# Scores' operand of a spectral and expert-retrieval kernel: float32 products in place of split bfloat16 products

## The chip, the cores and the metric

The kernel runs on one core of a Trainium2 chip. The metric is the device time of one execution in microseconds (us); the time before is 1265.43 us, the median of three runs (1265.05 to 1265.48). Five engines work side by side, each on a queue of its own that it goes through in order: TensorE (PE in the profile; its weight loads are shown apart as PEld), VectorE (DVE), ScalarE (ACT), GpSimd (POOL) and SyncE (SP), which here issues the DMAs. They wait for each other through semaphores.

## The reference, cut to what matters

Four sublayers, two kinds in turn, on 2048 tokens of 512 values: a Fourier mixing by DFT matrices, and a retrieval of experts by keys.

```python
q = jnp.einsum("nd,dhc->nhc", xf, w_q)      # w_q: (512, 32 heads, 2 * 128)
q1 = q[..., :dk]
q2 = q[..., dk:]
s1 = jnp.einsum("nhd,ed->nhe", q1, k1)      # k1, k2: (16, 128)
s2 = jnp.einsum("nhd,ed->nhe", q2, k2)
...
x = x + _A_ref(_layernorm(x, axis=-1), ...)   # y = Real(DFT_seq(DFT_hidden(x)))
x = x + _B_ref(_layernorm(x, axis=-1), ...)
x = x + _A_ref(_layernorm(x, axis=-1), ...)
x = x + _B_ref(_layernorm(x, axis=-1), ...)
```

The scores s1 and s2 of a token are its 512 values times w_q times the keys. The kernel never makes q. It first multiplies w_q by the keys, which gives one operand of 512 x (2 halves x 32 heads x 16 keys), and then multiplies the tokens by that operand. The two best of 16 scores are picked for each half and head, so the operand is kept to nearly float32 accuracy.

## The kernel before, in words

**Tiling.** Tokens lie in 16 tiles of 128. All products that need accuracy are made with operands held as a high and a low part (float32r, names ending in h and l): high x high, low x high, high x low. The DFT over the sequence goes by units of 256 tokens (`seq_unit`, from line 434): per unit 16 pieces of `cseq` are loaded by SP (`raw`, L454), split by ScalarE (`ch`, L458) and VectorE (`cl`, L462), and multiplied with the layer-normed tokens `xh`, `xl` on TensorE (L518, three products of 512 columns per step). The DFT over the hidden dimension (L615), the scores (L694, L698), the expert products and what follows are made token tile by token tile (`token_tile`).

**Set-up.** Before the first scores can be made, `setup` prepares the constants: the hidden DFT's matrices, the operand of the scores (`wh`, `wl`) and the experts' matrices. The operand is made from w_q in 32 groups of two heads of one half (16 groups for each of the two key matrices). A group is 512 KB in a tile `wr` (128 x 2 x 512 float32), loaded by SP (L315). For each group VectorE takes the upper 16 bits of each float32 as a bfloat16 part and subtracts it (L381, tile `w1`), then does that once more on what is left (L384). The keys have been split into three bfloat16 parts once (`kb`, 48 columns, L356 and L358). TensorE then visits the group: for each of 4 blocks of the model dimension and 2 heads it multiplies the three parts of w_q (as the weights, 128 x 128) with the 48 columns of the keys' parts, 24 products in all (L392). VectorE adds up the three key parts out of PSUM (L397, tile `ws`), ScalarE casts that to the high part (`wh`, L404) and VectorE subtracts to get the low part (`wl`, L407).

**What sets the order.** Every piece of work is an `Op` with an engine, an estimated duration, what it comes after, which buffers it takes and gives back, and a priority. `Plan.run` simulates the engines with these estimates and gives the order in which the instructions are issued; nothing is reordered afterwards. The durations are therefore no part of the arithmetic, but change the order. A visit of a group has the highest priority on TensorE once its inputs are planned to be there; sequence products fill the time between. Since each engine is in order, a visit whose inputs come later than planned holds up all the products that stand behind it. Buffers are counted in `BUFS`: five `wr` tiles, two sets of `wp` (`w1` and `ws`), four PSUM tiles `bank`, which the visits share with the token tiles, and four `acc` for the sequence DFT. The scores of the first token tile wait for all of the set-up (`setup_done`).

Other lines that are named below: L664 transposes a token tile's values (128 x 128 float32 through an identity), L725 multiplies them by the experts' operand (256 columns), L943 multiplies half-precision one-hot matrices in two column halves of the array, and L978, for the last token tile only, picks values with plain float32 products of 64 weight columns and 16 moving columns, in the same two halves.

Of the kernel before, what the change touches and what calls it, by code (L numbers as in the profile page):

```python
# [20 lines left out]
KD = D // P  # L21
# [3 lines left out]
SP = 1  # L25
NPC = NT // SP
NSC = 1
H = 32
E = 16
# [40 lines left out]
class Plan:  # L70
# [10 lines left out]
    def op(self, engine, us, fn, after=(), take=(), last=(), prio=(0, 0), lag=0.0, behind=()):  # L81
        o = Op(len(self.ops), engine, us, fn, [a for a in after if a is not None], list(take), list(last), prio, lag,
               list(behind))
        for h in o.last:
            h.users += 1
        self.ops.append(o)
        return o
# [59 lines left out]

MM512, MM256, TR32, TR16, MMG = 0.2275, 0.1203, 0.12, 0.057, 0.0156  # L150


def dve(n, rate=1):
    return 0.069 + n / (0.96e3 * rate)


def act(n):
    return 0.09 + n / 1.2e3


def load(kb):
    return kb / 256 * 1.05
# [3 lines left out]
def spectral_peer_kernel(ctx: ExitStack, tc, x_in, cseq, ctile, dhid, wq, k1t, k2t, ut, vm, out):  # L166
    nc = tc.nc
# [5 lines left out]
    ctx.enter_context(tc.manual_schedule())  # L173


    BUFS = {"acc": 4, "bank": 4, "raw": 4, "c": 3, "p": 1, "row": 4, "wr": 5, "wp": 2,
            "tok": 3, "sc": 1, "eq": 1, "act": 3, "q": 2, "top": 1, "qt": 1, "lr": 4, "gt": 1, "pp": 1, "gdr": 2, "bn": 1}
    plan = Plan(BUFS)

# [5 lines left out]
    wh = const.tile([P, KD, 2, H, E], F32R, name="wh")  # L185
    wl = const.tile([P, KD, 2, H, E], F32R, name="wl")
# [53 lines left out]
    def ln_stats(get, i, after, prio):  # L240
        bn, h = {}, Hold("bn")

        def f0():
            bn[0] = apool.tile([P, 6], F32, name="bn", bufs=BUFS["bn"])
            nc.vector.bn_stats(bn[0], get())
# [44 lines left out]
    xload = {}  # L290
    for i in range(NT):
        def first(i=i):
            h, t = Hold("wr"), {}

            def f():
                t[0] = setup_pool().tile([P, D], F32, name="wr", bufs=BUFS["wr"])
                nc.sync.dma_start(t[0], x_in[i * P:(i + 1) * P, :])
# [8 lines left out]
    setup_done = []  # L306

    def setup():
        def wr(src, prio, after):
            h, t = Hold("wr"), {}  # L310

            def f():
                t[0] = setup_pool().tile([P, 1024], F32, name="wr", bufs=BUFS["wr"]).rearrange(
                    "p (a b) -> p a b", b=src.shape[2])
                nc.sync.dma_start(t[0], src)  # L315

            return op("SP", load(512), f, [after], take=[h], prio=prio, lag=2.3), h, lambda: t[0]

        def parts(hi, lo, src, sign, prio):
            a, h, r = wr(src, prio, xload[8])  # L320

            def f0():
                if sign > 0:
                    nc.scalar.copy(hi, r())
                else:
                    nc.scalar.mul(hi, r(), -1.0)

            def f1():
                if sign > 0:
# [13 lines left out]


        kb, kready = [], []
        for hf, kt in enumerate((k1t, k2t)):
            kr = {}

            def f0(hf=hf, kt=kt, kr=kr):
                kr[0] = setup_pool().tile([P, 3, E], F32, name=f"kr{hf}")  # L350
                nc.sync.dma_start(kr[0][:, 0, :], kt)

            def f1(hf=hf, kr=kr):
                t = setup_pool().tile([P, 3, E], BF16, name=f"kb{hf}")
                for n in range(3):
                    nc.vector.tensor_copy(t[:, n, :], kr[0][:, n, :])  # L356
                    if n < 2:
                        nc.vector.tensor_sub(kr[0][:, n + 1, :], kr[0][:, n, :], t[:, n, :])  # L358
                kb.append(t)

            a = op("SP", 0.2, f0, prio=(1, hf), lag=2.3)
            kready.append(op("DVE", 0.9, f1, [a], prio=(1, hf)))


        HG = 2

        def halves(t, u):
            return t.bitcast(BF16).rearrange("p a (d u) -> p a d u", u=2)[:, :, :, u]

        def upper(t):  # L370
            return halves(t, 1)

        for hf in range(2):
            for g in range(H // HG):
                prio = (3, hf, g)
                a0, hw, r0 = wr(wq[hf, g * HG:(g + 1) * HG].rearrange("h c d -> c h d"), prio, xload[NT - 1])
                hp, hb, t = Hold("wp"), Hold("bank"), {}

                def f1(r0=r0, t=t):
                    t[1] = setup_pool().tile([P, HG, D], F32, name="w1", bufs=BUFS["wp"])  # L380
                    nc.vector.tensor_sub(t[1], r0(), upper(r0()))  # L381

                def f2(t=t):
                    nc.vector.tensor_sub(halves(t[1], 0), t[1], upper(t[1]))  # L384

                def f3(hf=hf, r0=r0, t=t):
                    t[3] = bank([P, KD * HG, 64])
                    ws = (upper(r0()), upper(t[1]), halves(t[1], 0))
                    for k in range(KD):
                        for a in range(HG):  # L390
                            for n, w in enumerate(ws):
                                nc.tensor.matmul(t[3][:, k * HG + a, :3 * E], w[:, a, k * P:(k + 1) * P],  # L392
                                                 kb[hf], start=(n == 0), stop=(n == 2), skip_group_check=True)

                def f4(t=t):
                    t[4] = setup_pool().tile([P, KD, HG, E], F32, name="ws", bufs=BUFS["wp"])
                    nc.vector.tensor_reduce(t[4].rearrange("p k a e -> p (k a) e"),  # L397
                                            t[3][:, :, :3 * E].rearrange("p b (n e) -> p b e n", e=E),
                                            axis=AX.X, op=ALU.add)

                hs = slice(g * HG, (g + 1) * HG)

                def f5(hf=hf, hs=hs, t=t):
                    nc.scalar.copy(wh[:, :, hf, hs, :], t[4])  # L404

                def f6(hf=hf, hs=hs, t=t):
                    nc.vector.tensor_sub(wl[:, :, hf, hs, :], t[4], as32(wh[:, :, hf, hs, :]))  # L407

                a1 = op("DVE", dve(1024), f1, [a0], take=[hp], prio=prio)
                a2 = op("DVE", dve(1024), f2, [a1], prio=prio)  # L410
                a3 = op("PE", 24 * 0.0255 + 0.1, f3, [a2, kready[hf]], take=[hb], last=[hw], prio=(0, 0))
                a4 = op("DVE", dve(384), f4, [a3], last=[hb], prio=prio)
                a5 = op("ACT", act(128), f5, [a4], prio=prio)
                setup_done.append(op("DVE", dve(128), f6, [a5], last=[hp], prio=prio))
        setup_done.append(parts(uh, ul, ut.rearrange("(k p) e -> p k e", p=P), 1, (4, 0)))
        setup_done.append(parts(vh, vl, vm.rearrange("(k p) e -> p k e", p=P), 1, (4, 1)))
        setup_done.extend(xready[0, i] for i in range(NT))
        return dft

    dft_done = setup()  # L420


# [138 lines left out]
    last = {}  # L561
# [629 lines left out]
```

## Time and profile before

| | |
|---|---|
| time, median of 3 runs | 1265.43 us (1265.05 to 1265.48) |
| time of the profiled execution | 1266.79 us |
| its span, first to last instruction | 1264.9 us |
| TensorE busy, longest group | L518, three groups of 1072 products, 398 to 408 us each |
| TensorE's granted clock | 1.00 throughout |
| visits of the changed code (L392) | 768 products, 58.8 to 181.8 us |
| loads of w_q (L315) | 32 of 512 KB, 4.1 us to landing |
| HBM read over the span | 107.36 MB |

A line of the grouped view names the kernel's line, the engine, the operation, the tiles (out<-in), the partitions and elements, and the count; then the busy time in us and the mean duration of one in ns; then the idle time of the engine just before, and what ended it. In the timeline the columns are start and duration in us, engine, line, operation, tiles and count, with the idle time before in brackets. The stretches give the busy time of each engine in us with its number of instructions, then TensorE's granted clock, the share of the DMA engines and GB/s. Products on TensorE overlap: one that shows 0.39 us is followed by the next after 0.23, so it is the step from start to start that counts, not the duration. PE busy is therefore near to full wherever products follow each other at any pace.

### The profile page before, as it was taken

The numbers are of one execution on the slowest core, as the hardware profiler recorded it, in microseconds if no ns is written. First come the engines' busy times: TensorE is split into PE (matmuls) and PEld (weight loads), VectorE is DVE, ScalarE is ACT, GpSimd is POOL, SyncE is SP. The second block draws the span as 40 slices with busy tenths as digits, with TensorE's granted clock in tenths as the row PEclk, the third lists the DMA queues.
The fourth block names the chain that finished last, engine by engine and source line by source line (L and its number), as shares of the span: only waits on it lengthen the run. The fifth ranks groups of instructions, "written<-read, shape, count | busy, mean of one in ns | idle before, by whom it ended". The sixth has DMA issues, their size and how long they took to land.

```text
span 1264.9 us, 20684 instructions
## 1 busy us (share of the span) xinstructions
PE 1250.8 (99%) x7804; PEld 1036.8 (82%) x7804; DVE 994.2 (79%) x2257; ACT 466.5 (37%) x966; POOL 45.7 (4%) x71
## 2 busy tenths in 40 slices
PE   9999999999999999999999999999999999999998
PEld 6777778887888888899878887888888888888886
DVE  8899998988887957779884378695685847778598
ACT  7522243343433333333563333333332433333232
POOL 2010000000000000000000000000000000000000
PEclk9999999999999999999999999999999999999999
DMA  7866541333233241413455204314142331414201
GB/s 235 268 197 213 180 150 34 92 70 65 67 84 76 76 101 50 112 39 88 121 133 135 67 26 104 81 59 109 42 108 51 93 91 51 108 43 110 58 9 35
DMA packets 224101, 121.18 MB, mean 96 GB/s; under 512 B 136448, under 2 KB 202496, under 8 KB 224000
## 3 DMA queue, kind: packets, MB, share of 16 engines
q1 hardware_dynamic: 224000, 119.85, 35.4%
q8 instruction: 61, 1.00, 0.3%
q14 instruction: 40, 0.33, 0.1%
HBM read 107.36 MB, written 12.45 MB: 95 GB/s over the span
## 4 chain that ended last, share of the span: by engine, by line
PE 71%; DVE 16%; issue 6%; DMA 2%; ACT 2%; SPq 1%; POOL 1%; POOLq 0%; DVEq 0%; ACTq 0%
PE acc L518 39%; PE bank L615 11%; PE bank L694 7%; PE bank L698 4%; PE bank L725 3%; DVE cl L462 2%; DVE w L384 2%; PE bank L1044 2%; DVE w L381 2%; PE bank L518 1%; PE bank L943 1%; DVE eq L778 1%; PE bank L1048 1%; PE bank L664 1%; POOL stats L260 1%
## 5 line engine op out<-in xcount | busy, mean ns | idle before, releaser
L518 PE MATMUL acc<-ch,xh 128*128 128x512 f32 (+1 forms) x1072 | 407.9, 381 | 0.0
L518 PE MATMUL acc<-ch,xl 128*128 128x512 f32 (+1 forms) x1072 | 397.8, 371 | 0.3 <-DVE xl L287 0.3
L518 PE MATMUL acc<-cl,xh 128*128 128x512 f32 (+1 forms) x1072 | 397.8, 371 | 0.0
L458 ACT CAST ch<-raw 128x512 fp32r<-128x512 f32 x256 | 158.4, 619 | 263.7 <-PE acc L518 227.0
L462 DVE TENSOR_TENSOR cl<-raw,ch 128x512 fp32r<-128x512 f32 x256 | 175.5, 687 | 72.4 <-ACT ch L458 52.9
L518 PEld LDWEIGHTS acc<-cl,xh 128*128 128x128 f32 x1072 | 201.9, 188 | 35.2
L518 PEld LDWEIGHTS acc<-ch,xh 128*128 128x128 f32 x1072 | 202.1, 189 | 32.6 <-issue 1.4
L518 PEld LDWEIGHTS acc<-ch,xl 128*128 128x128 f32 x1072 | 202.5, 189 | 31.6 <-DVE xl L287 1.0
L615 PE MATMUL bank<-dh,pth 128*128 128x512 f32 (+1 forms) x264 | 102.9, 392 | 0.4 <-ACT pth L543 0.4
L694 PE MATMUL bank<-wh,tok 128*128 128x512 f32 x256 | 100.2, 392 | 1.3 <-ACT sc L955 1.0
L615 PE MATMUL bank<-dl,pth 128*128 128x512 f32 (+1 forms) x264 | 100.6, 383 | 0.0
L694 PE MATMUL bank<-wl,tok 128*128 128x512 f32 x256 | 99.7, 390 | 0.0
L615 PE MATMUL bank<-dh,ptl 128*128 128x512 f32 (+1 forms) x264 | 95.9, 384 | 0.0
L784 DVE TENSOR_TENSOR tmp<-sc 128x512 f32<-128x512 f32 (+1 forms) x66 | 44.4, 672 | 61.7 <-ACT sc L703 60.8
L926 DVE TENSOR_TENSOR lr<-iota,qt 128x1024 f16<-128x1024 f16 x124 | 80.6, 684 | 10.6 <-ACT qt L907 10.6
L260 POOL TENSOR_TENSOR stats<-stats,half 128x1 f32<-128x1 f32 x64 | 44.4, 697 | 1183.7 <-DVE stats L257 1182.5
L778 DVE TENSOR_TENSOR eq<-sc,val 128x1024 f16<-128x1024 f32 (+1 forms) x66 | 78.5, 1190 | 1.5
L703 ACT COPY sc<-bank 128x512 f32<-128x512 f32 x64 | 36.8, 589 | 104.1 <-PE bank L698 73.1
L698 PE MATMUL bank<-wh,tok 128*128 128x512 f32 x256 | 68.5, 389 | 0.0
L800 DVE TENSOR_TENSOR eq<-eq 128x256 f16<-128x256 f16 (+3 forms) x198 | 60.0, 303 | 1.6
L615 PEld LDWEIGHTS bank<-dh,pth 128*128 128x128 f32 x264 | 49.6, 188 | 10.4 <-ACT pth L543 0.9
L694 PEld LDWEIGHTS bank<-wh,tok 128*128 128x128 f32 x256 | 48.1, 188 | 11.6 <-ACT raw L271 1.1
(152 smaller groups left out, 1790.7 us busy)
## 6 DMA issues: line engine op xcount, KB each, us to landing
raw<-in_cseq SPq DMA_DIRECT2D x224, 256.0 KB, 2.8
wr<-in_wq SPq DMA_DIRECT2D x32, 512.0 KB, 4.1
raw<-in_ctile SPq DMA_DIRECT2D x32, 256.0 KB, 2.9
wr<-in_x SPq DMA_DIRECT2D x16, 256.0 KB, 3.4
row<-in_x SPq DMA_DIRECT2D x16, 256.0 KB, 3.1
x2d<-row SPq DMA_DIRECT2D x16, 256.0 KB, 2.0
row<-x2d SPq DMA_DIRECT2D x16, 256.0 KB, 3.2
out<-row SPq DMA_DIRECT2D x16, 256.0 KB, 2.3
```

What stands on the lines that cost most here:

```text
L260: nc.gpsimd.tensor_tensor(st[:, 1:2], st[:, 1:2], half, op=ALU.pow)
L458: nc.scalar.copy(t[1], t[0])
L462: nc.vector.tensor_sub(t[2], t[0], as32(t[1]))
L518: nc.tensor.matmul(target(d), w[:, s, d * P:(d + 1) * P], moving(s % per, part), start=(s == 0 and k == 0 and d % blocks == 0), stop=(s == ...
L615: nc.tensor.matmul(t["y", cs.start], w[:, k, c, t0:t0 + P], r[:, c, k, cs], start=(z == 0 and c == 0 and m == 0), stop=(z == len(steps) - ...
L694: nc.tensor.matmul(t["pc", hf], t["th"][:, k, :], r[:, k, hf], start=(k == 0 and r is wh), stop=False)
L698: nc.tensor.matmul(t["pc", hf], t["tl"][:, k, :], wh[:, k, hf], start=False, stop=(k == KD - 1))
L725: nc.tensor.matmul(t["xu"], w[:, k, :], r[:, k, :], start=(m == 0), stop=(m == 3 * KD - 1))
L778: nc.vector.tensor_tensor(t["eq"][:, :, cols], flat("sc")[:, :, cols], val(rank_, cols), op=ALU.is_equal)
L784: nc.vector.tensor_max(t["tmp"][:, :, cols], flat("sc")[:, :8, cols], flat("sc")[:, 8:, cols])
L800: nc.vector.tensor_max(s[:, :m], s[:, :m], s[:, m:2 * m])
L926: nc.vector.tensor_tensor(t["m", hf, r], io2, row_of(r, hf), op=ALU.is_equal)
```

## The change

The operand's groups are multiplied in float32. The keys are kept as they are loaded (`kr`, 128 x 16 float32, for each half). Two groups of w_q (four heads) share one visit of TensorE: 4 heads x 4 blocks = 16 products with 128 columns of float32 weights straight from `wr` and 16 moving columns, into one PSUM tile. ScalarE casts the 256 values per partition to `wh` and VectorE subtracts to get `wl`, both directly from PSUM. The splitting of w_q and of the keys, the reduction and the tiles `w1`, `ws` and `kb` go. `wr` has seven buffers in place of five. There are 16 visits in place of 32, each planned at 16 x 0.105 us (`MM16`), where the old ones were planned at 24 x 0.0255 + 0.1.

```diff
-MM512, MM256, TR32, TR16, MMG = 0.2275, 0.1203, 0.12, 0.057, 0.0156
+MM512, MM256, TR32, TR16, MMG, MM16 = 0.2275, 0.1203, 0.12, 0.057, 0.0156, 0.105
...
-    BUFS = {"acc": 4, "bank": 4, "raw": 4, "c": 3, "p": 1, "row": 4, "wr": 5, "wp": 2,
+    BUFS = {"acc": 4, "bank": 4, "raw": 4, "c": 3, "p": 1, "row": 4, "wr": 7,
...
-            def f1(hf=hf, kr=kr):
-                t = setup_pool().tile([P, 3, E], BF16, name=f"kb{hf}")
-                for n in range(3):
-                    nc.vector.tensor_copy(t[:, n, :], kr[0][:, n, :])
-                    if n < 2:
-                        nc.vector.tensor_sub(kr[0][:, n + 1, :], kr[0][:, n, :], t[:, n, :])
-                kb.append(t)
...
-        HG = 2
+        HG, PG = 2, 2
...
-                def f1(r0=r0, t=t):
-                    t[1] = setup_pool().tile([P, HG, D], F32, name="w1", bufs=BUFS["wp"])
-                    nc.vector.tensor_sub(t[1], r0(), upper(r0()))
-
-                def f2(t=t):
-                    nc.vector.tensor_sub(halves(t[1], 0), t[1], upper(t[1]))
...
-                    for k in range(KD):
-                        for a in range(HG):
-                            for n, w in enumerate(ws):
-                                nc.tensor.matmul(t[3][:, k * HG + a, :3 * E], w[:, a, k * P:(k + 1) * P],
-                                                 kb[hf], start=(n == 0), stop=(n == 2), skip_group_check=True)
-
-                def f4(t=t):
-                    t[4] = setup_pool().tile([P, KD, HG, E], F32, name="ws", bufs=BUFS["wp"])
-                    nc.vector.tensor_reduce(t[4].rearrange("p k a e -> p (k a) e"),
-                                            t[3][:, :, :3 * E].rearrange("p b (n e) -> p b e n", e=E),
-                                            axis=AX.X, op=ALU.add)
...
+                def f0(hf=hf, loads=loads, t=t):
+                    t[0] = bank([P, KD, PG * HG, E])
+                    for m, (_, _, r) in enumerate(loads):
                         for a in range(HG):
+                            for k in range(KD):
+                                nc.tensor.matmul(t[0][:, k, m * HG + a], r()[:, a, k * P:(k + 1) * P], kr[hf],
+                                                 start=True, stop=True)
+
+                def f1(hf=hf, hs=hs, t=t):
+                    nc.scalar.copy(wh[:, :, hf, hs, :], t[0])
+
+                def f2(hf=hf, hs=hs, t=t):
+                    nc.vector.tensor_sub(wl[:, :, hf, hs, :], t[0], as32(wh[:, :, hf, hs, :]))
+
+                n = PG * HG * KD
+                a = op("PE", n * MM16, f0, [m[0] for m in loads] + [kready[hf]], take=[hb], last=[m[1] for m in loads],
+                       prio=(0, 0))
```

Below the change 32 lines are gone, so L518 is L486 there, L615 is L583, L454 is L422, L462 is L430; the new visit is L369, its casts L373 and its subtractions L376.

**TensorE, at the first visit** (about 58 us in the profile of before). Before, the last three products of a token tile's hidden DFT and the first two products of the visit, each with its own weight load; `wr` is the upper part of w_q, `w_683` the two others:

```order
L615 MATMUL bank<-dh,pth 128x512
L615 MATMUL bank<-dl,pth 128x512
L615 MATMUL bank<-dh,ptl 128x512
L392 LDWEIGHTS wr
L392 MATMUL bank<-kb_507,wr 128x48
L392 LDWEIGHTS w_683
L392 MATMUL bank<-kb_507,w_683 128x48
```

and of the change, the whole visit between the same neighbours (a float32 product loads its weights itself, so that no load is listed):

```order
L583 MATMUL bank<-dh,pth 128x512
L583 MATMUL bank<-dl,pth 128x512
L583 MATMUL bank<-dh,ptl 128x512
L369 MATMUL bank<-kr_452,wr 128x16 x16
L583 MATMUL bank<-dh,pth 128x512
```

A visit of 24 products of 48 columns becomes one of 16 products of 16 columns, for twice as many heads.

**VectorE, between two visits** (in the stage from 55 to 182 us of the profile of before). Before, what it does for one group and the next, with one split of a sequence piece (L462) between:

```order
L381 TENSOR_TENSOR w_929<-wr 128x1024
L397 TENSOR_REDUCE ws<-bank 128x128
L384 TENSOR_TENSOR w_929<-w_929 128x1024
L462 TENSOR_TENSOR cl<-raw,ch 128x512
L407 TENSOR_TENSOR wl<-ws,wh 128x4x32
L381 TENSOR_TENSOR w_981<-wr 128x1024
```

and of the change, in the same stage:

```order
L430 TENSOR_TENSOR cl<-raw,ch 128x512
L376 TENSOR_TENSOR wl<-bank,wh 128x4x64
L430 TENSOR_TENSOR cl<-raw,ch 128x512
L376 TENSOR_TENSOR wl<-bank,wh 128x4x64
L430 TENSOR_TENSOR cl<-raw,ch 128x512 x2
```

Four instructions per group are replaced by one for two groups; what is left between the splits of sequence pieces is the subtraction alone.

**SP, where the loads of w_q begin.** Before (`wr` from w_q, `raw` a piece of the sequence DFT's matrix):

```order
L315 DMA wr<-in_wq 128x2x512 x6
L454 DMA raw<-in_cseq 128x2x256
L315 DMA wr<-in_wq 128x2x512
L454 DMA raw<-in_cseq 128x2x256
L315 DMA wr<-in_wq 128x2x512
```

and of the change:

```order
L315 DMA wr<-in_wq 128x2x512 x8
L422 DMA raw<-in_cseq 128x2x256
L315 DMA wr<-in_wq 128x2x512 x2
L422 DMA raw<-in_cseq 128x2x256
L315 DMA wr<-in_wq 128x2x512 x2
L422 DMA raw<-in_cseq 128x2x256
L315 DMA wr<-in_wq 128x2x512
```

The loads of w_q stand closer together in the queue: over all 32 of them, 18 pieces of the sequence matrix lie between the first and the last where 27 did, and as before two rows of tokens.

More of the change, by code (lines that the diff above doesn't have):

```diff
@@ L342, in setup @@
                                  dhid[c].rearrange("(k p) e -> p k e", p=P)[:, ks, :], 1 - 2 * c, (2, c, k)))
-        kb, kready = [], []
+        kr, kready = [], []
         for hf, kt in enumerate((k1t, k2t)):
[L347 to L351, printed above, removed]
-            def f1(hf=hf, kr=kr):
-                t = setup_pool().tile([P, 3, E], BF16, name=f"kb{hf}")
-                for n in range(3):
-                    nc.vector.tensor_copy(t[:, n, :], kr[0][:, n, :])
-                    if n < 2:
-                        nc.vector.tensor_sub(kr[0][:, n + 1, :], kr[0][:, n, :], t[:, n, :])
-                kb.append(t)
-            a = op("SP", 0.2, f0, prio=(1, hf), lag=2.3)
-            kready.append(op("DVE", 0.9, f1, [a], prio=(1, hf)))
@@ L365, in setup, with f0 @@
-        HG = 2
[L367 to L371, printed above, removed]
+            def f0(hf=hf, kt=kt):
+                kr.append(setup_pool().tile([P, E], F32, name=f"kr{hf}"))
+                nc.sync.dma_start(kr[hf], kt)
+            kready.append(op("SP", 0.2, f0, prio=(1, hf), lag=2.3))
+        HG, PG = 2, 2
         for hf in range(2):
-            for g in range(H // HG):
+            for g in range(0, H // HG, PG):
@@ L375, in setup @@
                 prio = (3, hf, g)
-                a0, hw, r0 = wr(wq[hf, g * HG:(g + 1) * HG].rearrange("h c d -> c h d"), prio, xload[NT - 1])
-                hp, hb, t = Hold("wp"), Hold("bank"), {}
-                def f1(r0=r0, t=t):
-                    t[1] = setup_pool().tile([P, HG, D], F32, name="w1", bufs=BUFS["wp"])
-                    nc.vector.tensor_sub(t[1], r0(), upper(r0()))
-                def f2(t=t):
-                    nc.vector.tensor_sub(halves(t[1], 0), t[1], upper(t[1]))
@@ L386, in f3 @@
-                def f3(hf=hf, r0=r0, t=t):
-                    t[3] = bank([P, KD * HG, 64])
-                    ws = (upper(r0()), upper(t[1]), halves(t[1], 0))
-                    for k in range(KD):
-                        for a in range(HG):
-                            for n, w in enumerate(ws):
-                                nc.tensor.matmul(t[3][:, k * HG + a, :3 * E], w[:, a, k * P:(k + 1) * P],
-                                                 kb[hf], start=(n == 0), stop=(n == 2), skip_group_check=True)
@@ L395, in f4 @@
-                def f4(t=t):
-                    t[4] = setup_pool().tile([P, KD, HG, E], F32, name="ws", bufs=BUFS["wp"])
-                    nc.vector.tensor_reduce(t[4].rearrange("p k a e -> p (k a) e"),
-                                            t[3][:, :, :3 * E].rearrange("p b (n e) -> p b e n", e=E),
-                                            axis=AX.X, op=ALU.add)
-                hs = slice(g * HG, (g + 1) * HG)
-                def f5(hf=hf, hs=hs, t=t):
-                    nc.scalar.copy(wh[:, :, hf, hs, :], t[4])
@@ L406, in f6 @@
[L406 to L413, printed above, removed]
@@ L414, in setup @@
-                setup_done.append(op("DVE", dve(128), f6, [a5], last=[hp], prio=prio))
+                loads = [wr(wq[hf, m * HG:(m + 1) * HG].rearrange("h c d -> c h d"), prio, xload[NT - 1])
+                         for m in range(g, g + PG)]
+                hb, t = Hold("bank"), {}
+                hs = slice(g * HG, (g + PG) * HG)
+                def f0(hf=hf, loads=loads, t=t):
+                    t[0] = bank([P, KD, PG * HG, E])
+                    for m, (_, _, r) in enumerate(loads):
+                        for a in range(HG):
+                            for k in range(KD):
+                                nc.tensor.matmul(t[0][:, k, m * HG + a], r()[:, a, k * P:(k + 1) * P], kr[hf],
+                                                 start=True, stop=True)
@@ new lines, in f1 @@
+                def f1(hf=hf, hs=hs, t=t):
[5 more added lines that the diff above has]
+                       prio=(0, 0))
+                a = op("ACT", act(n * E), f1, [a], prio=prio)
@@ L415, in setup @@
+                setup_done.append(op("DVE", dve(n * E), f2, [a], last=[hb], prio=prio))
         setup_done.append(parts(uh, ul, ut.rearrange("(k p) e -> p k e", p=P), 1, (4, 0)))
```

## Prediction

> **What bounds the kernel now.** I read the page's busy shares first, then the busy time by stretch around the place of the change, then the chain of waits there, then the timeline of TensorE at one visit of the changed code.
>
> ```profile
> span 1264.9 us, 20684 instructions
> ...
> PE 1250.8 (99%) x7804; PEld 1036.8 (82%) x7804; DVE 994.2 (79%) x2257; ACT 466.5 (37%) x966; POOL 45.7 (4%) x71
> ```
> ```profile
> core 0: us, PE busy (x) PEld busy (x) DVE busy (x) ACT busy (x) POOL busy (x), PEclk, DMA share, GB/s
> 55.00:182.00 127.00, 125.42 (x1207) 99.89 (x1206) 123.90 (x180) 29.81 (x65) 5.86 (x4) 1.00 0.63 199
> 182.00:400.00 218.00, 216.54 (x1258) 176.50 (x1258) 188.88 (x465) 84.37 (x187) 8.28 (x12) 1.00 0.29 70
> ```
> ```profile
> by line: DVE w L384 21.8%; PE acc L518 18.5%; DVE w L381 18.1%; DVE cl L462 7.9%; DVE ws L397 6.3%; DMA wr<-in_wq 5.0%; issue 4.7%; PE bank L392 4.6%; POOL stats L260 4.2%; DVE wl L407 3.4%; DVE bn L245 2.0%; DVE ptl L546 1.8%; DVE row L625
> ```
>
> The changed code runs from 55 to 182 us. There the chain (restricted to that stretch) goes mostly through VectorE: L384 and L381, the splitting of w_q. That looks like a VectorE bound. The row above it says otherwise for the end of the kernel: TensorE is busy 125.4 of 127 us in the same stretch, because it fills the time between two visits with sequence products (L518) that must be done anyway. TensorE's work is one in-order queue of fixed total. So the rule that I use: the end moves by what TensorE spends on the operand, waits inside its visits included, and VectorE's saving is worth only the waits of TensorE that it takes away. At the most that is the idle time: 1.6 us here and 1.5 us in the stretch behind it.
>
> **What TensorE pays now.** The timeline of TensorE at a visit that waits for nothing (start, duration):
>
> ```profile
> 58.52 0.39 PE L615 MATMUL bank<-dh,ptl 128*128 128x512 f32 x1
> 58.76 0.20 PE L392 MATMUL bank<-kb,wr 128*128 128x48 bf16 x1
> ...
> 59.32 0.21 PE L392 MATMUL bank<-kb,w 128*128 128x48 bf16 x2
> 59.37 0.48 PE L615 MATMUL bank<-dh,pth 128*128 128x512 f32 x1
> 59.68 0.40 PE L615 MATMUL bank<-dl,pth 128*128 128x512 f32 x1
> ```
> and at one that waits:
> ```profile
> 90.05 0.39 PE L518 MATMUL acc<-cl,xh 128*128 128x512 f32 x1
> 90.28 0.20 PE L392 MATMUL bank<-kb,wr 128*128 128x48 bf16 x1
> ...
> 91.13 0.47 PE L518 MATMUL acc<-ch,xh 128*128 128x512 f32 x1
> 91.44 0.39 PE L518 MATMUL acc<-ch,xl 128*128 128x512 f32 x1
> ```
>
> From 58.52 to 59.68 is 1.16 us. Two ordinary steps of a 512-column product would take 0.45 of it (91.44 less 91.13 is a slow one; 58.52 to 58.76 an ordinary one, 0.23). So the quiet visit costs 0.71: 24 products from 58.76 to 59.37, 0.61 or 0.025 each, and 0.10 for getting in and out. The waiting visit costs 1.39 - 0.45 = 0.94. Over all 32:
>
> ```profile
> 55.00:182.00 127.00, 27.68 (x768) 22.56 (x768) 1.00 0.63 199
> ```
> ```profile
> L392 PE MATMUL bank<-kb,w 128*128 128x48 bf16 x512 | 26.4, 183 | 1.6 <-DVE w L384 0.8
> L392 PEld LDWEIGHTS <-w 128*128 128x128 bf16 x512 | 22.1, 97 | 3.3 <-DVE w L384 2.6 <-DVE stats L257 0.2
> ```
>
> The first row is line L392 alone: TensorE busy 27.7 us. Add the 1.6 idle ahead of its products, and take off 0.06 per visit (a quiet visit shows busy until 59.32 + 0.21, that is 0.77, and costs 0.71), 1.9 in all: **27.4 us**. Without waits it would be 32 x 0.71 = 22.7; so VectorE's splitting costs TensorE some 4.7 us, and that is all that goes with it.
>
> **What TensorE will pay.** 16 visits of 16 float32 products, each with 128 columns of weights and 16 moving columns. No row of before is such a product. The nearest in type and moving columns is L978, with 64 columns of weights:
>
> ```profile
> L978 PEld LDWEIGHTS bank<-picks,pth x64: 133/138/138, 1255.6 to 1257.4; 128*64 128x64 f32 x64
> L978 PE MATMUL bank<-picks,pth x64: 209/209/230, 1255.6 to 1257.5; 128*64 128x16 f32 x64
> ```
> ```profile
> 1255.64 1.95 PEld L978 LDWEIGHTS bank<-picks,pth 128*64 128x64 f32 x64 [0.56 <-DVE pth L969]
> ```
> ```profile
> 1255.69 0.20 PEld L978 LDWEIGHTS bank<-picks,pth 128*64 128x64 f32 x4
> ```
>
> The code issues 32 products at L978 (16 x 2); the profile has 64 loads and 64 products. **A plain float32 product is two loads and two products.** So 256 products become 512 loads. The last row shows four loads within 0.20 us where one takes 0.138: they start in pairs, 0.06 apart. The two halves of the array (j = 0 and 1, 64 columns each) load side by side; each half takes a new load every (1.95 - 0.14) / 31 = 0.058 us. A full-width product has no second half to run beside it. What a load of 128 float32 columns takes, the loads say:
>
> ```profile
> L943 PEld LDWEIGHTS <-lr x256: 106/113/113, 220.8 to 398.1; 128*64 128x64 f16 x128
> ```
> ```profile
> L518 PEld LDWEIGHTS acc<-ch,xh x1072: 186/188/192, 17.4 to 1221.6; 128*128 128x128 f32 x179
> ```
> ```profile
> L664 PEld LDWEIGHTS bank<-identf,tok x128: 138/140/144, 186.0 to 1231.1; 128*128 128x128 f32 x128
> ```
> ```profile
> 53.19 0.19 PEld L518 LDWEIGHTS acc<-ch,xh 128*128 128x128 f32 x1 [0.29 <-issue]
> 53.30 0.19 PEld L518 LDWEIGHTS acc<-ch,xl 128*128 128x128 f32 x1
> ```
> ```profile
> 185.97 0.14 PEld L664 LDWEIGHTS bank<-identf,tok 128*128 128x128 f32 x1 [0.26 <-ACT tok L271]
> ```
> ```profile
> 186.03 0.14 PEld L664 LDWEIGHTS bank<-identf,tok 128*128 128x128 f32 x1
> ```
>
> After a wait, when nothing else paces them, L518's loads (float32r, 128 columns) follow each other after 0.11 us, L664's (float32, 128 columns, but a transpose) after 0.06. L978's took 0.058 for half the columns, with the duration of L664's. From 64 columns (0.138) to L518's 128 (0.188) the duration grows by 0.050, as a load whose time goes with its columns would: 0.058 for 64, 0.11 for 128. L943's 64 columns of two bytes take 0.113, less than four bytes' 0.138. So I take L978 and L518 as one kind and L664's transpose as another, and **0.11 us per load, 0.22 per product**; the 16 moving columns hide behind the loads. A visit: 16 x 0.22 + 0.10 = 3.62; all: 16 x 3.62 = **57.9 us**. Bounds: 0.108 per load (the 0.11 row, rounded down) gives 56.9; 0.12, the step of 256-column products, gives 63.0; L664's 0.06 and L978's pace per issued product are the rivals below.
>
> ```profile
> 1237.46 0.28 PE L725 MATMUL bank<-ul,tok 128*128 128x256 f32 x1
> 1237.58 0.28 PE L725 MATMUL bank<-uh,tok 128*128 128x256 f32 x1
> ```
>
> Against the row of L392 (97 ns a load, a product every 25) stands a rule of the Trainium skill, "TensorE: Matmul & The Clock Gate", section "Weight-path perf modes — Fast Weight Load (FWL) and DoubleRow": full-width weights get a fast load only if their type is not FP32. By it the removed bfloat16 loads were fast ones and the new ones are not; the section "LDWEIGHTS (loading the stationary operand)" gives columns / 1.2 ns, an estimate of 107 ns for 128 columns, and a sum of 16 x (16 x 0.213 + 0.10) = 56.2 us. The trace agrees with it at L518 (0.11) and not at L664 (0.06).
>
> **VectorE, ScalarE, DMA.** What leaves VectorE and what comes:
>
> ```profile
> L384 DVE TENSOR_TENSOR w<-w 128x1024 bf16<-128x1024 f32 x32 | 44.5, 1389 | 0.1
> L381 DVE TENSOR_TENSOR w<-wr 128x1024 f32<-128x1024 f32 x32 | 39.3, 1228 | 1.4 <-DMA wr<-in_wq 1.4
> L397 DVE TENSOR_REDUCE ws<-bank 128x128 f32<-128x384 f32 x32 | 18.0, 561 | 0.0
> L407 DVE TENSOR_TENSOR wl<-ws,wh 128x128 fp32r<-128x128 f32 x32 | 9.4, 294 | 0.4 <-ACT wh L404 0.4
> ```
> ```profile
> L1031 DVE TENSOR_TENSOR pl<-bank,ph 128x256 fp32r<-128x256 f32 x31 | 12.9, 417 | 8.5 <-ACT ph L1027 8.4
> ```
>
> Out go 111.2 us; in come 16 subtractions like L1031, 6.7 us: VectorE loses 104 us. By the rule above this is worth the 4.7 us already counted, and 0 to 1.5 us behind 182 us (I take 0: VectorE's 189 of 218 us there is the tokens' own work, not a backlog). ScalarE's casts halve in number; it idles anyway. The visit now waits for two loads, not for VectorE; behind it on TensorE stand the sequence products. SP's queue holds the same 32 loads of w_q, with 18 sequence pieces and 2 rows between the first and last in place of 27 and 2: 22 MB. Between first and last visit the order has 237 full products, 54 us, plus the visits' 58: 112 us, 196 GB/s, under this row's 254:
>
> ```profile
> 50.00:60.00 10.00, 10.00 (x66) 8.02 (x65) 7.69 (x9) 3.76 (x6) 0.00 (x0) 1.00 0.78 254
> ```
>
> So transfers stay hidden, at no cost. Sum: 57.9 - 27.4 = **+30.5 us**. The profiled execution took 1266.8 us (span 1264.9), the median of the runs is 1265.4; on the median the forecast is **1296 us**, its own range 1292 (less 1.5 recovered behind, loads of 0.108) to 1301 (loads of 0.12).
>
> **Rivals.** (1) *Full-width plain float32 loads run like L664's*, at 0.0575: 0.115 per product, 16 x (1.84 + 0.10) = 31.0, +3.6: 1269. For it: L664 alone has both the type and the width. Against it: L664 is a transpose, has one load per product where L978 has two, and L978's 64 columns would then be expected below 0.058. The visits then span 54 + 31 = 85 us, 259 GB/s, just over the 254, so up to 2 us of waits for w_q may come on top; 1.5 us recovered behind may go off. 1264 to 1271. A variant, with 0.05 of this rival's chance: the loads hide altogether and a product goes by steps of L392's 0.025, four of them: 0.10, in all 16 x (1.6 + 0.10) = 27.2, no change; L978's 0.058 for a pair of half-width loads speaks against it, since 0.05 would have done. The Trainium skill has the rule for this variant: "FP8 and Floating Point Precision", section "TensorE Precision Notes", says that true FP32 takes four passes, and "TensorE: Matmul & The Clock Gate", section "Wait — 56ns, not 53.3ns?", that no product starts sooner than about 25 ns after the last. The trace agrees on the 25 ns (24 products in 0.61 us), and no run here shows the four. (2) *Faster:* the pace of L978 per issued product (1.95 / 32, less the first, 0.058) holds at full width too, its pairs being the two halves of one product rather than two products side by side. Then 16 x (0.93 + 0.10) = 16.4, -11.0: 1254. The point is 0.10 us per product, (27.4 / 16 - 0.10) / 16; below it the change gains. Against it: two loads into the same columns would have to run at once.
>
> **How the numbers follow.** Forecast 0.60; rival 1 0.25; rival 2 0.08; 0.07 for prices between or waits that I don't see. The range must take in rival 1 and leaves out rival 2: 1263 to 1301. What differs by over 0.2% (2.5 us) a measurement of this kernel can tell from no change. Slower: 0.60, half of rival 1 (0.13), and 0.06 of the rest, 0.79; same: 0.10 of rival 1 and 0.01, 0.11; faster: 0.08 and 0.02, 0.10.
>
> **What would show it.** After: 512 loads and 512 products at the new line, loads 0.11 apart within a visit; TensorE busy about 58 us on it; visits of 3.6 us; no wait for w_q over 1 us in all. Loads 0.06 apart mean rival 1, 0.03 rival 2. VectorE should fall by 104 us. The forecast is wrong if the loads are shorter, or if a stall outside 55 to 182 us grows by more than 3 us.

## Result: 1317 us, 4% slower, and the profile after

The changed kernel takes **1317.07 us** (median of 4 runs, 1313.0 to 1318.21) against 1265.24 us (1264.87 to 1265.48): a ratio of 1.0404, 95% interval [1.0382, 1.0427], or +51.8 us. The forecast was 1296 us with a range of 1263 to 1301: the side was right, the size was not. The profiled execution took 1313.0 us, +46.2 on the one of before. The page of after, with the row of TensorE's granted clock:

```profile
span 1311.1 us, 20037 instructions
...
PE 1299.1 (99%) x7548; PEld 1088.1 (83%) x7548; DVE 910.0 (69%) x2135; ACT 466.4 (36%) x950; POOL 43.6 (3%) x71
...
PEclk9988979999999999999999999999999999999999
```

TensorE is as busy as before, and VectorE has lost 84 us. New is the last line: **the clock** is at 90% or more in every slice of before,

```profile
PEclk9999999999999999999999999999999999999999
```

and below that in slices 3, 4 and 6 of the change (a slice is 32.8 us), which is where the visits are. The visits themselves are what was forecast. First the new line's instructions (durations in ns, lowest, median, highest), then TensorE's timeline at the first visit and its loads in a short window:

```profile
L369 PEld LDWEIGHTS bank<-kr,wr x512: 187/192/338, 59.6 to 184.4; 128*128 128x128 f32 x171
L369 PE MATMUL bank<-kr,wr x512: 177/263/376, 59.8 to 184.5; 128*128 128x16 f32 x171
```
```profile
59.59 0.39 PE L583 MATMUL bank<-dh,ptl 128*128 128x512 f32 x1
59.82 3.64 PE L369 MATMUL bank<-kr,wr 128*128 128x16 f32 x32
63.31 0.49 PE L583 MATMUL bank<-dh,pth 128*128 128x512 f32 x1
63.63 0.40 PE L583 MATMUL bank<-dl,pth 128*128 128x512 f32 x1
```
```profile
59.82 0.52 PEld L369 LDWEIGHTS bank<-kr,wr 128*128 128x128 f32 x4
```

256 products are 512 loads. Four loads in 0.52 us, of which one lasts 0.19, are 0.11 apart. The visit costs 63.63 - 59.59 - 0.45 = 3.59 us; sixteen of these are 57.4. Against the forecast's +30.5 that leaves some 16 us of the profiled execution, and 21 of the median, that the sum does not have. They are mostly in the rows between the visits, a few microseconds further on:

```profile
64.14 0.63 PE L583 MATMUL bank<-dh,pth 128*128 128x512 f32 x1
64.56 0.63 PE L583 MATMUL bank<-dl,pth 128*128 128x512 f32 x1
64.99 0.63 PE L583 MATMUL bank<-dh,ptl 128*128 128x512 f32 x1
```

These are ordinary products of 512 columns that wait for nothing, and they step by 0.43 us, not 0.23. In the trace the granted clock changes only after 3.41 us or whole multiples of it (but for the start and the end of the execution). Laid over that grid, line L369 alone shows what decides (stretch, its length; TensorE busy on the line in us and instructions; the loads; granted clock in that stretch; DMA share; GB/s):

```profile
core 0: us, PE busy (x) PEld busy (x), PEclk, DMA share, GB/s
60.62:64.04 3.42, 2.84 (x26) 2.74 (x25) 1.00 1.03 373
64.04:67.45 3.41, 0.00 (x0) 0.00 (x0) 0.50 0.97 367
67.45:70.87 3.42, 3.12 (x29) 3.31 (x29) 1.00 0.09 35
70.87:74.28 3.41, 0.87 (x5) 0.76 (x4) 0.50 0.45 149
74.28:77.69 3.41, 2.02 (x19) 2.21 (x20) 1.00 0.02 5
77.69:81.10 3.41, 1.62 (x15) 1.52 (x14) 1.00 0.00 0
81.10:84.52 3.42, 3.18 (x30) 3.37 (x30) 1.00 0.14 39
84.52:87.93 3.41, 0.75 (x5) 0.64 (x4) 0.50 0.96 338
87.93:91.35 3.42, 2.08 (x20) 2.27 (x20) 1.00 0.02 8
```

Read each row with the next one's clock. After a stretch with 2.84, 3.12 or 3.18 us of the visit in it comes one at 0.50; after 2.02, 1.62 and 2.08 the clock stays (the row after 87.93 is not shown; its clock is 1.00). A visit of 3.6 us is longer than a stretch, so how much of one stretch it takes up depends on where it falls. The whole stage as one row:

```profile
55.00:200.00 145.00, 145.00 (x833) 128.10 (x833) 31.36 (x60) 23.75 (x44) 2.19 (x4) 0.88 0.46 156
```

A mean clock of 0.88 over 145 us is 17 us of clock lost, and 30.0 (57.4 - 27.4) + 17 = 47 against the measured 46.2. The other runs lost more clock and more time: mean granted clock 0.987 at 1313.0 us, 0.983 at 1317, 0.982 at 1318.2.

### The profile page after: what moved, and what is told of

It is laid out like the page before. It is cut to its first block, busy times and chain, and to the rows that moved or that the text cites. A ratio compares the mean times of both kernels' runs of the same rounds, so it can differ in the third digit from the quotient of the medians.

```text
span 1311.1 us, 20037 instructions
## 1 busy us (share of the span) xinstructions
PE 1299.1 (99%) x7548; PEld 1088.1 (83%) x7548; DVE 910.0 (69%) x2135; ACT 466.4 (36%) x950; POOL 43.6 (3%) x71
## 4 chain that ended last, share of the span: by engine, by line
PE 83%; DVE 8%; issue 5%; DMA 2%; ACT 1%; SPq 1%; POOL 1%; POOLq 0%; ACTq 0%; DVEq 0%
PE acc L486 44%; PE bank L583 13%; PE bank L662 7%; PE bank L369 4%; PE bank L666 3%; PE bank L693 3%; PE bank L1012 2%; PE bank L486 1%; PE bank L911 1%; PE bank L1016 1%; DVE cl L430 1%; DVE eq L746 1%; PE bank L632 1%; SPq L967 1%; PE acc L466 1%
## 5 line engine op out<-in xcount | busy, mean ns | idle before, releaser
L486 PE MATMUL acc<-ch,xh 128*128 128x512 f32 (+1 forms) x1072 | 409.4, 382 | 0.1
L486 PE MATMUL acc<-ch,xl 128*128 128x512 f32 (+1 forms) x1072 | 400.8, 374 | 0.0
L486 PE MATMUL acc<-cl,xh 128*128 128x512 f32 (+1 forms) x1072 | 400.6, 374 | 0.0
L430 DVE TENSOR_TENSOR cl<-raw,ch 128x512 fp32r<-128x512 f32 x256 | 175.9, 688 | 114.0 <-ACT ch L426 85.8
L486 PEld LDWEIGHTS acc<-cl,xh 128*128 128x128 f32 x1072 | 203.8, 190 | 35.9
L486 PEld LDWEIGHTS acc<-ch,xh 128*128 128x128 f32 x1072 | 204.2, 190 | 34.4 <-issue 1.9
L486 PEld LDWEIGHTS acc<-ch,xl 128*128 128x128 f32 x1072 | 204.0, 190 | 32.0 <-DVE xl L287 0.4
L583 PE MATMUL bank<-dh,pth 128*128 128x512 f32 (+1 forms) x264 | 105.4, 401 | 0.4 <-ACT pth L511 0.4
L583 PE MATMUL bank<-dl,pth 128*128 128x512 f32 (+1 forms) x264 | 103.3, 393 | 0.0
L583 PE MATMUL bank<-dh,ptl 128*128 128x512 f32 (+1 forms) x264 | 98.6, 394 | 0.0
L369 PEld LDWEIGHTS bank<-kr,wr 128*128 128x128 f32 x512 | 61.5, 196 | 1.4
L583 PEld LDWEIGHTS bank<-dh,pth 128*128 128x128 f32 x264 | 51.3, 194 | 10.8 <-ACT pth L511 0.9
```

Source lines behind the costliest of these rows:

```text
L369: nc.tensor.matmul(t[0][:, k, m * HG + a], r()[:, a, k * P:(k + 1) * P], kr[hf], start=True, stop=True)
L430: nc.vector.tensor_sub(t[2], t[0], as32(t[1]))
L486: nc.tensor.matmul(target(d), w[:, s, d * P:(d + 1) * P], moving(s % per, part), start=(s == 0 and k == 0 and d % blocks == 0), stop=(s == ...
L583: nc.tensor.matmul(t["y", cs.start], w[:, k, c, t0:t0 + P], r[:, c, k, cs], start=(z == 0 and c == 0 and m == 0), stop=(z == len(steps) - ...
```

## The experiments

Theory G: the 16 columns that hide behind 0.11 us of loading leave the array idle for most of a visit. Where that takes up enough of a stretch of 3.41 us, TensorE counts as idle to whatever grants its clock, and the clock is halved for the next stretch, for all products. Rival O: the order, made with 0.105 us per product, is what costs the extra time. Each kernel was timed over several runs beside the kernel before on the same chip (1265 to 1266 us there).

| run | median us | range | ratio to before, 95% interval | clock of the profiled run |
|---|---|---|---|---|
| the change | 1317.07 | 1313.0 to 1318.2 | 1.0404 [1.0382, 1.0427] | 0.987 |
| half_visits | 1302.25 | 1297.4 to 1305.1 | 1.0281 [1.0257, 1.0306] | 0.993 |
| wide96 | 1296.14 | 1295.2 to 1296.6 | 1.0234 [1.0217, 1.0252] | 1.000 |
| wide32 | 1310.40 | 1305.2 to 1315.8 | 1.0350 [1.0316, 1.0384] | 0.984 |
| plan022 | 1345.68 | 1340.9 to 1348.6 | 1.0625 [1.0598, 1.0652] | 0.959 |
| half96 | 1296.92 | 1296.2 to 1297.5 | 1.0244 [1.0228, 1.0259] | 1.000 |
| one_product | 1248.29 | 1247.3 to 1249.6 | 0.9870 [0.9853, 0.9886] | 0.999 |
| no_split | 1260.20 | 1259.5 to 1261.3 | 0.9964 [0.9950, 0.9977] | 1.000 |
| pool_split | 1279.05 | 1278.5 to 1279.3 | 1.0112 [1.0097, 1.0127] | 0.998 |
| pool_split2 | 1266.89 | 1265.9 to 1267.9 | 1.0014 [1.0005, 1.0024] | 1.000 |
| two_parts | 1254.25 | 1253.9 to 1254.5 | 0.9906 [0.9890, 0.9923] | 1.000 |

**wide96: the same visits, the array in use.** The moving columns are read six times over; each product's surplus is overwritten by the next.

```diff
-                                nc.tensor.matmul(t[0][:, k, m * HG + a], r()[:, a, k * P:(k + 1) * P], kr[hf],
+                                at = (k * PG * HG + m * HG + a) * E
+                                nc.tensor.matmul(t[1][:, at:at + 6 * E], r()[:, a, k * P:(k + 1) * P], rep,
                                                  start=True, stop=True)
```

with `rep = kr[hf][:, None, :].to_broadcast([P, 6, E])`, and the loop over k outermost so that the columns follow each other.

> The change with every product's 16 moving columns given six times over (96 columns; what they write beyond the first 16 is overwritten by the next product). Same order, same visits, same weight loads. If the loads pace a product, as the 0.112 us steps say, the visit stays at 3.6 us, and if theory G is right the array is used some 0.16 of every 0.22 us, so the clock is not cut: 1265.3 - 27.4 + 16 x 3.6 = 1296 us, clock 1.00. Rival O: nothing of the order has changed, 1313 to 1318. Rival P (the columns are not hidden behind the loads): visits grow by 16 x 0.13 us to 5.7 us, and the time to 1345.

1296.14 us. The page's clock row and the new line:

```profile
PEclk9999999999999999999999999999999999999999
```
```profile
L372 PEld LDWEIGHTS bank<-kr,wr x512: 187/192/192, 59.4 to 170.8; 128*128 128x128 f32 x171
L372 PE MATMUL bank<-kr,wr x512: 243/275/275, 59.7 to 170.9; 128*128 128x96 f32 x171
```

The loads never go above 192 ns (338 in the change), so no visit ran at half clock, and six times the columns cost nothing. TensorE's products stand in the order of the change line by line, and the loads are as many and as long. Besides the use of the array, the blocks change places within a visit and the PSUM tile is longer; wide32 (next) shares both and is still cut. The columns take away 20.9 us (1317.07 to 1296.14; 22.1 if each is taken against before on its own chip, 51.8 - 29.7) and leave the forecast's sum. Rivals O and P fall.

**wide32: the same with 32 columns.**

```diff
-                    rep = kr[hf][:, None, :].to_broadcast([P, 6, E])
+                    rep = kr[hf][:, None, :].to_broadcast([P, 2, E])
```

> As wide96, with the 16 columns given twice (32). Theory G with a threshold on how much the array is used: between the change and wide96, since a visit uses the array for about a quarter of the time in place of an eighth; only stretches that lie almost wholly inside a visit would still be cut, about half of them: 1300 to 1310 us, clock 0.990 to 0.995. If the clock goes by waiting or by instructions and not by columns: as the change, 1313 to 1318.

1310.4 us, between the two as expected, though at the upper end, and the clock was cut more than I had put it: 0.984 in the profiled run (1315.8 us), 0.988, 0.991 and 0.992 in the others, the fastest of which took 1305.2. Twice the columns help only in part: in its trace 2.64 us of the visits in a stretch leave the clock at full and 2.81 us cut it, where 2.50 us are enough in the change (the last section has the row).

**half_visits: the same products in visits half as long.**

```diff
-        HG, PG = 2, 2
+        HG, PG = 2, 1
```

> The change with one group per visit: 32 visits of 8 float32 products, the same 256 products. Theory G (a stretch of 3.4 us of the clock's grid that lies for over two thirds inside a visit makes the next stretch run at half clock): a visit lasts 8 x 0.224 + 0.1 = 1.9 us, no stretch fills up, the granted clock stays at 1.00, and only the loads' price is left: 1265.3 - 27.4 + 32 x 1.9 = 1299 us. Rival O (the order made with 0.105 us per product is what costs the extra 17 to 21 us, through stalls): the order is still made with 0.105, so 1313 to 1318.

1302.25 us, between the two, because the order did not do what I expected of it. In one run the clock stayed at 1.00: 1297.4, G's value. In the profiled one (1305.1):

```profile
70.66 0.39 PE L583 MATMUL bank<-dh,ptl 128*128 128x512 f32 x1
70.89 4.46 PE L369 MATMUL bank<-kr,wr 128*128 128x16 f32 x32
75.19 0.77 PE L583 MATMUL bank<-dh,pth 128*128 128x512 f32 x1
75.76 0.63 PE L583 MATMUL bank<-dl,pth 128*128 128x512 f32 x1
```
```profile
70.08:73.49 3.41, 3.41 (x30) 3.25 (x28) 0.42 (x2) 0.27 (x1) 0.00 (x0) 1.00 0.44 159
73.49:90.56 17.07, 17.07 (x65) 15.33 (x64) 3.36 (x9) 1.42 (x4) 0.55 (x1) 0.50 0.00 0
90.56:200.00 109.44, 109.44 (x685) 97.65 (x686) 30.03 (x63) 26.96 (x58) 2.03 (x2) 1.00 0.48 157
```

Two visits stand side by side, 32 products' records in one row. That one pair takes up 2.60 us of a stretch; then the clock stays at half for 17 us, five stretches. Three of these six stretches, line L369 alone:

```profile
70.08:73.49 3.41, 2.60 (x25) 2.79 (x25) 1.00 0.44 159
80.32:83.73 3.41, 1.00 (x5) 1.18 (x6) 0.50 0.00 0
83.73:87.14 3.41, 3.27 (x16) 3.31 (x16) 0.50 0.00 0
```

At half clock a load's step is 0.21 us, so a visit of 8 takes twice as long, and less of a visit is enough to keep the clock down: after the second row, with 1.00 us of it, the clock is still at half. **The cut sustains itself** until the visits are far enough apart. The rest, 110 us of visits of 1.80 us each with products between, is at full clock.

**half96: both together.** half_visits with the 96 columns.

> half_visits with the 16 columns given six times, as in wide96. In half_visits two visits that the order puts side by side cut the clock in three runs of four (1302 to 1305; 1297.4 in the one whose clock stayed at 1.00). Theory G: with the array in use no stretch is cut whatever lies side by side: visits of 1.80 us, 1265.2 - 27.4 + 32 x 1.80 = 1295.4 us, clock 1.00 in every run. If something else made half_visits slower than its sum (more waits at twice as many visits): 1300 to 1305.

1296.92 us, clock 1.000 in all four runs. With the array in use the pairs do no harm, and twice as many visits cost only what the sum says (by the timeline 57.3 us in all, and 57.2 in wide96).

**plan022: the planner's price corrected.**

```diff
-MM512, MM256, TR32, TR16, MMG, MM16 = 0.2275, 0.1203, 0.12, 0.057, 0.0156, 0.105
+MM512, MM256, TR32, TR16, MMG, MM16 = 0.2275, 0.1203, 0.12, 0.057, 0.0156, 0.22
```

> The change with the planner's price of a product set to 0.22 us in place of 0.105; the same instructions in another order. Theory G: visits of 3.6 us as before, the clock is cut as before: 1310 to 1320 us. Rival O: with the right price the stalls go, 1296 us.

1345.68 us: rival O is out by 50 us in the wrong direction, and my own figure is 26 to 36 us too low. With the longer price the planner sets visits in pairs:

```profile
92.03 13.67 PE L369 MATMUL bank<-kr,wr 128*128 128x16 f32 x64
```
```profile
60.00:83.20 23.20, 23.20 (x140) 22.04 (x139) 2.78 (x8) 1.31 (x4) 0.55 (x1) 0.71 0.69 224
83.20:158.30 75.10, 75.10 (x321) 71.91 (x321) 6.82 (x16) 4.47 (x12) 0.55 (x1) 0.50 0.41 128
158.30:182.20 23.90, 23.90 (x113) 22.45 (x112) 4.62 (x7) 3.94 (x8) 0.00 (x0) 0.57 0.24 77
```

A pair that takes 7.2 us at full clock takes 14 at half, and the clock stays at 0.50 for 75 us without a break. It is the mechanism of half_visits, carried further. Only the order differs from the change, and TensorE never waits in these rows (busy in all of each stretch).

**one_product: is it TensorE's spending that moves the end?** One product of 256 columns per visit.

```diff
+                    rep = kr[hf][:, None, :].to_broadcast([P, KD * PG * HG, E])
+                    nc.tensor.matmul(t[0].rearrange("p k a e -> p (k a) e"), loads[1][2]()[:, 0, :P], rep, start=True, stop=True)
```

> The change with one product per visit in place of 16: 16 visits of one product of 256 moving columns, which fills all that is read afterwards. It leaves out 15 of 16 products, so the scores' operand is not the reference's. The rule of the prediction (the end moves by what TensorE spends on the operand, nothing else): two loads and twice 256 columns, 16 x (0.43 + 0.10) = 8.5 us; 1265.3 - 27.4 + 8.5 = 1246 us (1244 to 1248), clock 1.00. Rival V (VectorE's 104 us shorten the end too, since the chain of waits of before goes through VectorE): below 1240.

1248.29 us, 2 us above the value and far from rival V. The visits came out at 0.44 us each, not 0.53, but two of them waited:

```profile
  DMA wr<-in_wq: 1.5, 2
  PE acc L483: 0.5, 1
```

These are the waits of the line's engine (us, times); with them the visits cost 8.2 us in all, so the 2 us are not in the visits, and I did not trace them further.

**no_split: what VectorE's splitting costs.** It leaves out L381 and L384; the upper part stands for all three.

```diff
-                    ws = (upper(r0()), upper(t[1]), halves(t[1], 0))
+                    ws = (upper(r0()),) * 3
```

> The kernel before without VectorE's two splitting steps (83.8 us of L381 and L384): the upper part of w_q stands for all three parts, so the operand is less accurate. TensorE's 768 bfloat16 products and the loads are as before. The rule of the prediction: only the waits inside the visits go, 4.7 us: 1260.6 us (1259 to 1263). Rival V (VectorE bounds that stage): tens of us less, below 1245.

1260.20 us, -5.0 against 4.7 expected. By the timeline its visits cost 22.8 us in all, where those of before cost 27.4. 84 us of VectorE's work in the stage where the chain of waits named VectorE are worth 5 us of time.

**pool_split and pool_split2: one splitting step on GpSimd.** Nothing is left out.

```diff
-                    nc.vector.tensor_sub(t[1], r0(), upper(r0()))
+                    nc.gpsimd.tensor_sub(t[1], r0(), upper(r0()))
...
-                a1 = op("DVE", dve(1024), f1, [a0], take=[hp], prio=prio)
+                a1 = op("POOL", 2.4, f1, [a0], take=[hp], prio=prio)
```

> The kernel before with the first splitting step (L381) on GpSimd in place of VectorE, nothing left out. VectorE gets 39 us back in the stage. If GpSimd does 1024 elements in under 3 us (a visit comes every 3.6 us), the waits inside the visits shrink by up to 4.7 us: 1261 to 1264. If GpSimd is slower than that, or slows VectorE by sharing its way to memory, visits wait for it: 1266 or more.

> As pool_split, with the second splitting step (L384, 44.5 us) on GpSimd and the first on VectorE, nothing left out. Visits wait for the second step, so its length on GpSimd counts directly where the planner's order has little room: 1261 to 1264 if it takes under 2.4 us as planned, 1266 or more if longer.

1279.05 and 1266.89 us: misses. GpSimd does take less than was planned, 2.17 us (1.22 on VectorE):

```profile
L381 POOL TENSOR_TENSOR w<-wr x32: 1888/2174/2737, 51.9 to 186.3; 128x1024 f32<-128x1024 f32 x32
L381 POOLq EVENT_SEMAPHORE  x30: 42/1146/6368, 60.2 to 180.4; - x30
its engine sat idle before it (us, times) until:
  PE bank L392: 48.6, 15
```
```profile
PEld L392 <- DVE w L384: 12.0, 10, 1.6
PE bank L392 <- DVE w L384: 10.9, 10, 1.5
```

In pool_split GpSimd waits for a buffer until the visit before has given it back (first fence), then the longer chain GpSimd, VectorE, TensorE ends in the visit's waits: 10.9 us of idle TensorE in place of 0.8 (second fence, waits of 55 to 190 us). VectorE is slowed as well. Two of its lines from 55 to 182 us:

```profile
L407 DVE TENSOR_TENSOR wl<-ws,wh 128x128 fp32r<-128x128 f32 x28 | 27.5, 987 | 3.8 <-ACT wh L404 3.7
L397 DVE TENSOR_REDUCE ws<-bank 128x128 f32<-128x384 f32 x28 | 15.3, 549 | 1.5 <-PE bank L392 1.3
```

The subtraction L407, which reads two tiles, took 294 ns in before and takes 987 on average here; L462 goes from 696 to 1046. The reduction L397, which reads PSUM alone, is as fast as before (561). So the 39 us that VectorE gives away come back as longer instructions (its busy time is 998.6 us in all, 994.2 before); what the two engines contend for is not shown. pool_split2 gives 0.14% more than before, [0.05%, 0.24%]: nothing gained. GpSimd's step takes 2.21 us there, under the 2.4 planned, but three visits wait 3.8 us for it, and L407 takes 852 ns.

**two_parts: a version that beats both, for less accuracy.** w_q in two bfloat16 parts; the third, and with it L384, is left out.

```diff
-                    ws = (upper(r0()), upper(t[1]), halves(t[1], 0))
+                    ws = (upper(r0()), upper(t[1]))
```

> The kernel before with w_q in two bfloat16 parts in place of three: the third part is left out (16 upper bits of w_q's fraction and sign are kept in all, the keys keep three parts). TensorE has 16 products a visit in place of 24 (256 x 0.025 = 6.4 us less) and VectorE has no L384 (44.5 us less), so the 4.7 us of waits inside the visits go too: 1265.2 - 6.4 - 4.7 = 1254 us. If the waits stay (VectorE still the last in the stage): 1259.

1254.25 us, -0.94% [-1.10%, -0.77%]: 11.8 us less than before on the same chip, where the two terms, TensorE's products and its waits, gave 11.1.

## Why the prediction was wrong in size

- **"The end moves by what TensorE spends on the operand, waits inside its visits included."** Right as to VectorE (no_split, two_parts), and nearly so at one_product. But it was used as if products outside the visits kept their pace. Here the visits slowed those, too.
- **27.4 us now, 4.7 of it waits.** no_split took away 5.0 of the time and 4.6 of the visits. Right.
- **"A plain float32 product is two loads and two products", 0.11 us per load.** Right: 512 records, steps of 0.11, a visit of 3.59 against 3.62. The choice between the two nearest rows, L518's 0.11 and L664's 0.06, fell on the right side; rivals 1 and 2 are out. wide96 isolates this term with the clock held: +29.7 us on the runs of the same chip (1296.14 - 1266.4) against +30.5. One bound was added up wrong: 1265.4 + 56.9 - 27.4 - 1.5 is 1293.4, not 1292; the stated range does not rest on it.
- **"The 16 moving columns hide behind the loads."** This is the step that failed. In time they do hide, as wide96 shows with 96. What they leave behind is an array that is idle while its queue is full, and the sum has no term for the clock. The row of the granted clock was on the page of before, at full in all slices, and I carried it over without asking what keeps it there. The missing term is 20.9 us (1317.07 - 1296.14). A sign of it was there: a forecast visit of 3.6 us, nearly all of it loading, is longer than the one spell of narrow float32 products that before has, L978's 1.95 us.
- The Trainium skill has the rule that I passed over: "TensorE: Matmul & The Clock Gate", section "Part 1: The HAM clock gate (the "warmup" mystery)", describes a free-running window of 3413 ns, after which the clock is halved when the array has not been busy. The trace agrees on the length (rows 3.41 us apart) and on the half clock (0.50), and adds what counts as idle: not a waiting queue alone, but also a visit of narrow float32 products.
- **VectorE loses 104 us.** The busy share shows 84, since back-to-back instructions overlap and the groups count the overlap twice (the durations alone add up to 102.5 us less). It did not matter to the time.
- **Transfers stay hidden.** Right; no product waited for w_q in the visits of the change. The bound, 254 GB/s, was no limit: 373 GB/s stands in the grid's first row.
- **0 to 1.5 us regained behind 182 us.** Not resolved; the sum closes within a microsecond without it.

## What to carry to other kernels

When products are paced by their weight loads, price two things: the loads, which the nearest rows of the same width give well, and the share of time in which columns stream. A spell of mostly loading that takes up some 2.5 us of a 3.41 us stretch slowed everything in the next stretch here, so keep such spells short and apart, or use the hidden time for more columns. Where TensorE's queue is always full, an engine that leads the chain of waits in a stage may still be worth only the idle time of TensorE, here 5 us of 84.

## What was not expected of the hardware

- The clock is cut with TensorE's queue full: 2.50 us of a 3.41 us stretch in narrow float32 products is enough, 2.08 is not. In the change, line L369 alone:

```profile
139.13:142.55 3.42, 2.50 (x23) 2.40 (x22) 1.00 0.67 227
142.55:145.96 3.41, 0.00 (x0) 0.00 (x0) 0.50 0.63 217
```

- Weight loads go by the same clock: their step is 0.11 us at full and 0.21 at half, and once the clock is down less of a visit keeps it there, so the cut feeds on itself (17 us in half_visits from one pair, 75 us in plan022). In the change it does so once, after a stretch with 1.31 us of the last visit:

```profile
183.51:186.92 3.41, 1.31 (x7) 1.21 (x6) 0.50 0.00 0
186.92:190.33 3.41, 0.00 (x0) 0.00 (x0) 0.50 0.00 0
```

- One limit fits all of these cuts. As an estimate, count the moving columns that TensorE takes in during each stretch, from the starts and shapes of the records in all twelve traces. A plain float32 product's columns count twice, since one_product's 256 cost 0.22 us a record where L725's 256 cost 0.12. Leaving out the first 8 us and the last 4 us of each trace, 60 of 4480 stretches are followed by half clock. Every stretch with fewer than about 2980 columns is among them, and none with more than about 3030, whether the stretch itself ran at full or at half clock. Ordinary products bring some 7700 columns in a stretch at full clock (0.23 us for 512) and some 4100 at half (0.43 us), which is why less of a visit keeps the clock down than cuts it. Plain waiting counts alike: the one cut of pool_split, at 293 us, follows a stretch in which TensorE stood idle for 2.45 us.
- With 32 columns per product the clock is still cut (0.984 to 0.992), with 96 it is not. No width between the two was run.
